# Single-bank PSUM ring, output pieces 18 slices behind and later recurrent reads in a cross-attention and ReGLU kernel

## The chip, the cores and the metric

The kernel runs on one core of a Trainium2 chip. The profiles call the engines PE (TensorE, the matmuls; PEld are its weight loads), ACT (ScalarE), DVE (VectorE), POOL (GpSimd) and SP (SyncE). PSUM is the memory into which the matmuls of this kernel write; ACT and DVE copy the results from there. The metric is the device time of one execution in microseconds, as the median of the runs. The span that the profile gives is about 2 us shorter than the time of the same run. Ratios use runs in the fast state alone; medians and ranges are over all runs of a kernel, of which one in experiment 3 (272.96 us, the split copies) was in the slow state.

## The reference, cut to what matters

```python
# x: 8 batches, 8 heads, 512 tokens, 64 wide; state: 8 batches, 8 heads, 32 slots, 64 wide
a     = softmax(x @ state.T / 8)     ; xread = a  @ state     # 512 tokens read the state
a2    = softmax(state @ x.T / 8)     ; sread = a2 @ x         # 32 slots read the tokens
rows  = concat(xread, sread)         # heads joined: 8 * 544 rows of 512
out   = (relu(rows @ w_gate) * (rows @ w_val)) @ w_out        # 512 -> 1536 -> 512
```

Both kernels avoid `xread` itself: they form U = state @ w_gate and state @ w_val per batch, so that `rows @ w_gate` becomes `a @ U`. Per batch there are

- 12 **slices**: 128 columns of d_ff, two matmuls for gate and two for val, each 128x512; then a relu on ACT and a product on DVE (`h_sb`);
- 12 **pieces**: four 128x512 matmuls each; three pieces make one output tile of 128 rows;
- **units**: scores and their normalisation, transposes, U blocks, and the recurrent reads (`sr`).

## The kernel before

Both kernels allot eight banks of PSUM. In the old one they are a ring of three tiles of two banks, one output bank, and one bank for everything else. A tile is handed on as a whole: its next user waits until the last reader of the tile is done, as the waits below show.

```python
    ps_gv = pool("ps_gv", 3, PS)          # 3 tiles [128, 2, 512]: slices, U, xT, stT
    ps_o = pool("ps_o", 1, PS)            # output tiles
    ps_m = pool("ps_m", 1, PS)            # scores, recurrent reads, aT and srT transposes
    ...
    def gv(b, jf):
        ...
        ps = ps2("gv_ps")                 # gate in ps[:, 0], val in ps[:, 1]
    ...
    def u_block(b, lo, engs=("act", "dve")):
        u_alloc(b)
        for w in range(2):
            ps = ps2("up")
            u_mm(ps, b, w, lo, 512)
            copy[engs[w]](out=U[b][:, w, :, lo:lo + 512], in_=ps)    # 1024 columns at once
    ...
    # startup, in this order on TensorE
    sr0 = sr_mm(0, 0)                     # a recurrent read, held in a PSUM tile until sr_norm
    state_prep(2, 5)
    u_chunk(0, 0)
    u_chunk(1, 0, "dve")
    sr_norm(0, 0, sr0)
    att_aT_pe(0, 0, "act")                # needs the single bank of sr0
    ...
    gv_full(0, 0)
    ...                                   # all 24 slices of batches 0 and 1, then:
    for s in range(2, B + 1):             # stage s: slices of batch s, pieces of batch s-2
        ...
        if n < B:                         # n = s + 1: units of the next batch
            for i, jf in enumerate((3, 5, 7, 9, 10)):
                u.setdefault(jf, []).append(lambda i=i: att_unit_dma(n, i))
            for i, jf in enumerate((4, 6, 8)):
                u.setdefault(jf, []).append(lambda i=i: u_block(n, 512 * i))
```

The softmax here doesn't subtract the row's maximum and nothing guards it: scores larger than these inputs give would overflow.

## Time and profile before

| | before |
|---|---|
| median of three runs | 270.2 us (268.87 to 270.82) |
| span in the profile | 270.1 us |
| first slice starts | 17.4 us |
| first output piece | 68.2 us |
| pitch of stages 3 to 6 | 26.24 us |

The starts of slices in this document are counted: a slice has four weight loads from U, and the timeline lists every weight load. The pitch is the distance between the first slices of two batches. The profiled run is another one, of 271.92 us, with a mean granted clock of 0.975.

From the page of the old kernel, the parts on engines and on forty slices of the span (busy tenths; PEclk is the granted clock in tenths):

```profile
span 270.1 us, 4360 instructions
...
PE 231.8 (86%) x1759; PEld 113.7 (42%) x1790; DVE 140.6 (52%) x250; ACT 129.2 (48%) x215; POOL 25.5 (9%) x36
...
PE   7656667786599788889988998899889999999993
...
PEclk9958889999889999999999999999999999999999
...
```

PE is nearly full in the second half and far from it in the first third. The clock drops in the third of these forty slices and again later.

The waits of PE (who waited for whom: us, times, longest), first from 0 to 82 us, then from 82 to 250 us:

```profile
...
PE gv_ps L279 <- ACT U L269: 4.8, 4, 1.2
PE xT_ps L166 <- ACT xT L169: 2.9, 4, 0.8
PE aT_ps L206 <- DVE br L239: 2.6, 1, 2.6
PE aT_ps L206 <- DVE sr_sb L225: 2.5, 1, 2.5
...
```

```profile
...
PE gv_ps L279 <- DVE h_sb L299: 9.3, 11, 1.0
...
```

The first list holds two kinds of waits for PSUM. `xT` waits for a copy of the other half of its own two-bank tile. `aT` waits for whoever holds the single bank: at 15.83 us for the recurrent read, at 71.84 us for `br`. The timeline at the first of these (start, duration, engine, line, operation, tiles, and in brackets the idle time before and what ended it):

```profile
...
13.75 1.21 DVE L269 CAST U<-upc 128x1024 bf16<-128x1024 f32 x1
...
15.06 0.71 DVE L225 TENSOR_SCALAR sr_sb<-sr_ps,rr 64x128 bf16<-64x128 f32 x2
...
15.83 0.61 PE L206 MATMUL aT_ps<-id_94,a_sn 128*128 128x128 bf16 x4 [2.53 <-DVE sr_sb L225]
...
```

The read's normalisation stands behind a U copy of 1.21 us on DVE, and PE stands still for 2.53 us; the copy, a reciprocal and the normalisation itself fill 2.0 us of them. The clock falls as well. These are windows of 2 us with their granted clock (the column after POOL):

```profile
...
core 0: us, PE busy (x) PEld busy (x) DVE busy (x) ACT busy (x) POOL busy (x), PEclk, DMA share, GB/s
...
12.00:14.00 2.00, 1.08 (x38) 0.71 (x38) 1.93 (x6) 0.26 (x2) 0.74 (x2) 1.00 1.45 196
14.00:16.00 2.00, 0.17 (x2) 0.17 (x3) 1.73 (x4) 1.45 (x3) 1.14 (x2) 0.71 1.45 195
16.00:18.00 2.00, 1.78 (x10) 1.09 (x10) 0.00 (x0) 0.82 (x2) 1.08 (x2) 0.50 1.45 198
...
```

In the stages, the timeline shows one kind of gap only, next to a U block:

```profile
...
138.76 0.69 DVE L190 TENSOR_TENSOR a_sn<-e_sn,rc 128x512 bf16<-128x512 bf16 x1
138.96 0.40 PE L254 MATMUL up<-wv_sb,stT 64*32 64x512 bf16 x8
139.22 1.01 ACT L262 CAST U<-up 128x1024 bf16<-128x1024 f32 x1 [0.64 <-PE up L254]
...
139.36 0.69 DVE L299 TENSOR_TENSOR h_sb<-gv_ps,g_sb 128x512 bf16<-128x512 f32 x1
...
140.10 1.02 PE L279 MATMUL gv_ps<-ans,U 128*128 128x512 bf16 x4 [0.74 <-DVE h_sb L299]
...
```

The U block took two of three tiles. The next slice needs the third, which held the slice before, and that is free only after its product (139.36 to 140.05 us), which stood behind a normalisation on DVE (138.76). A stage has two such gaps, 0.74 us here and 0.99 us at the next U block.

### The profile page before, as it was taken

Reading aid. Unit: us, or ns where it says so; the run is one execution under the profiler, and the core shown is the slowest. Engines: PE = TensorE matmul, PEld = TensorE weight load, DVE = VectorE, ACT = ScalarE, POOL = GpSimd, SP = SyncE. Lnnn points to the kernel's source line nnn. Section 1 sums busy time; section 2 is a strip of 40 time slices with the busy share of each in tenths; the row PEclk is TensorE's granted clock in tenths of the full one; section 3 lists DMA queues with packets and bytes.
Section 4 is the critical chain, followed back from the end, with each engine's and each line's share of the span. In section 5 each row is a group of like instructions: output and inputs, shape, how many; then the busy total and the mean of one; then the engine's idle time right before and its main releaser. Section 6 shows DMA issues by size and latency. Waiting matters only on the chain.

```text
span 270.1 us, 4360 instructions
## 1 busy us (share of the span) xinstructions
PE 231.8 (86%) x1759; PEld 113.7 (42%) x1790; DVE 140.6 (52%) x250; ACT 129.2 (48%) x215; POOL 25.5 (9%) x36
## 2 busy tenths in 40 slices
PE   7656667786599788889988998899889999999993
PEld 2423323343344343344434444344435444666442
DVE  3634634556556876677467647763776433222000
ACT  3344666664336653554454555455645444333211
POOL 4853002000003002000300020000000000000000
PEclk9958889999889999999999999999999999999999
DMA  7999994000061193139114911641131211111242
GB/s 211 195 196 196 205 242 79 4 0 2 0 187 48 39 188 125 39 88 259 44 41 111 241 41 40 137 60 39 41 78 39 78 41 39 54 67 39 78 119 78
DMA packets 38388, 25.71 MB, mean 95 GB/s; under 512 B 18784, under 2 KB 33888, under 8 KB 38368
## 3 DMA queue, kind: packets, MB, share of 16 engines
q1 hardware_dynamic: 27248, 17.70, 24.4%
q0 software_dynamic: 10256, 6.82, 16.1%
q10 hardware_dynamic: 864, 0.92, 1.2%
q8 instruction: 14, 0.23, 0.4%
q14 instruction: 6, 0.05, 0.1%
HBM read 18.35 MB, written 8.91 MB: 101 GB/s over the span
## 4 chain that ended last, share of the span: by engine, by line
PE 68%; DVE 18%; ACT 11%; issue 2%; DVEq 0%; ACTq 0%
PE o_ps L311 27%; PE gv_ps L279 27%; DVE h_sb L299 6%; PE gvs_ps L289 4%; ACT g_sb L295 4%; DVE a_sn L190 4%; DVE cs L187 4%; ACT e_sn L182 3%; PE sr_ps L214 3%; ACT U L269 2%; PE warm_ps L355 2%; DVE rc L189 1%; ACT xT L169 1%; PE o_ps L337 1%; PE up L254 1%
## 5 line engine op out<-in xcount | busy, mean ns | idle before, releaser
L279 PE MATMUL gv_ps<-ans,U 128*128 128x512 bf16 x359 | 98.6, 389 | 19.0 <-DVE h_sb L299 9.7
L299 DVE TENSOR_TENSOR h_sb<-gv_ps,g_sb 128x512 bf16<-128x512 f32 x96 | 66.3, 691 | 72.2 <-ACT g_sb L295 72.2
L311 PE MATMUL o_ps<-wo_sb,h_sb 128*128 128x512 bf16 x367 | 94.8, 382 | 0.3
L295 ACT ACTIVATE g_sb<-gv_ps 128x512 bf16<-128x512 f32 x96 | 57.3, 597 | 71.0 <-PE gv_ps L279 68.3
L279 PEld LDWEIGHTS <-U 128*128 128x128 bf16 x384 | 35.2, 99 | 60.3 <-issue 21.7
L311 PEld LDWEIGHTS <-h_sb 128*128 128x128 bf16 x372 | 36.5, 99 | 40.8 <-issue 0.7
L319 ACT COPY o_sb<-o_ps 128x512 f32<-128x512 f32 x31 | 18.2, 586 | 16.5 <-PE o_ps L311 16.5
L262 DVE CAST U<-up 128x1024 bf16<-128x1024 f32 x18 | 21.9, 1218 | 1.2 <-PE up L254 0.6
L146 POOL CAST xb<-xf 128x1024 bf16<-128x1024 f32 x10 | 10.1, 1041 | 123.9 <-DMA xf<-in_x_dram 123.9
L262 ACT CAST U<-up 128x1024 bf16<-128x1024 f32 x18 | 18.2, 1014 | 7.5 <-PE up L254 7.5
L187 DVE TENSOR_REDUCE cs<-e_sn 128x16 f32<-128x512 bf16 x16 | 10.9, 683 | 6.9 <-ACT e_sn L182 6.9
L299 DVE TENSOR_TENSOR hs_sb<-gvs_ps,g_sb 128x256 bf16<-128x256 f32 x12 | 5.1, 425 | 15.3 <-ACT g_sb L295 15.3
L182 ACT ACTIVATE e_sn<-sc_ps 128x512 bf16<-128x512 f32 x16 | 9.6, 597 | 4.9 <-PE sc_ps L180 4.9
L269 ACT CAST U<-upc 128x1024 bf16<-128x1024 f32 x11 | 11.0, 1015 | 1.8 <-PE upc L254 1.8
L225 DVE TENSOR_SCALAR sr_sb<-sr_ps,rr 64x128 bf16<-64x128 f32 x32 | 11.2, 349 | 0.8
L190 DVE TENSOR_TENSOR a_sn<-e_sn,rc 128x512 bf16<-128x512 bf16 x16 | 11.1, 692 | 0.6
L214 PE MATMUL sr_ps<-xb,e_sn 128*128 128x256 bf16 x64 | 11.3, 278 | 0.0
L295 ACT ACTIVATE g_sb<-gvs_ps 128x256 bf16<-128x256 f32 x12 | 4.6, 384 | 12.0 <-PE gvs_ps L289 12.0
L254 PEld LDWEIGHTS <-stT 64*32 64x32 bf16 x480 | 4.6, 89 | 11.6 <-issue 11.1
L216 PE MATMUL sr_ps<-ones,e_sn 128*128 128x1 bf16 x64 | 9.4, 168 | 0.0
L340 DVE COPY o_sb<-o_ps 128x256 f32<-128x256 f32 x1 | 0.4, 424 | 16.3 <-PE o_ps L337 16.3
L254 PE MATMUL up<-wg_sb,stT 64*32 64x512 bf16 x144 | 7.4, 386 | 0.9 <-DVE h_sb L299 0.9
(61 smaller groups left out, 150.1 us busy)
## 6 DMA issues: line engine op xcount, KB each, us to landing
out_dram<-o_sb SPq DMA_DIRECT2D x31, 256.0 KB, 2.3
xf<-in_x_dram SPq DMA_DIRECT2D x4, 1024.0 KB, 6.5
wg_sb<-in_moe_w_gate_dram POOLq DMA_DIRECT2D x6, 256.0 KB, 10.0
wv_sb<-in_moe_w_val_dram POOLq DMA_DIRECT2D x6, 256.0 KB, 10.1
wo_sb<-in_moe_w_out_dram POOLq DMA_DIRECT2D x2, 768.0 KB, 16.1
xb<-in_x_dram POOLq DMA_DIRECT2D x2, 512.0 KB, 9.4
xf<-in_x_dram POOLq DMA_DIRECT2D x1, 1024.0 KB, 18.8
xf<-in_x_dram ACTq DMA_DIRECT2D x1, 512.0 KB, 4.4
```

The lines of the kernel that those rows point to most:

```text
L182: nc.scalar.activation(out=e_sn[b][:, kc].rearrange("p c m -> p (c m)"), in_=t, func=AF.Exp, scale=scale)
L187: nc.vector.reduce_sum(out=cs, in_=e_v, axis=AX.X)
L190: nc.vector.tensor_tensor(out=a_sn[b][:, kc].rearrange("p c (h n) -> p (c h) n", n=Ns), in0=e_v, in1=rc.to_broadcast([128, NC * HK, Ns]), ...
L214: nc.tensor.matmul(ps[:, 0:256], e_sn[b][:, kc, c], xb[b][:, c, HK * kc:HK * kc + HK], start=(c == 0), stop=(c == NC - 1), skip_group_chec ...
L254: nc.tensor.matmul(ps[q:q + 32, kc, 0:n], stT[r:r + 64, b, j, 32 * sl:32 * sl + 32], wsb[r:r + 64, j, lo:lo + n], start=True, stop=True)
L262: copy[engs[w]](out=U[b][:, w, :, lo:lo + 512], in_=ps)
L269: copy[eng](out=U[b][:, :, :, lo:lo + 256].rearrange("p w k f -> p k w f"), in_=ps)
L279: nc.tensor.matmul(ps[:, w], U[b][:, w, kc, f0:f0 + 128], ANS[b][:, kc].rearrange("p c t -> p (c t)"), start=(kc == 0), stop=(kc == NK - 1))
L295: nc.scalar.activation(out=g_sb[:, 0:n], in_=ps[:, 0, 0:n], func=AF.Relu)
L299: nc.vector.tensor_tensor(out=dst, in0=ps[:, 1, 0:n], in1=g_sb[:, 0:n], op=ALU.mult)
L311: nc.tensor.matmul(o_ps[0], src[:, jf, tsub * 128:(tsub + 1) * 128], wo_sb[:, jf], start=(jf == 0), stop=(jf == NF - 1))
L319: nc.scalar.copy(out=o_sb, in_=o_ps[0])
```

## The change

The intent: one stream of slices in which pieces follow 18 slices behind, with no break between startup and stages; PSUM as a ring of six single banks and two output banks, so that a bank comes free as soon as its one reader is done; and recurrent reads of the first batches moved to stage 2, where DVE has time. The U copies are split, as a tile is now one bank. The exponentials of the scores (`e_sn`) get a third buffer, as the reads that use them come later. The loads of batch 0 come in quarters, and the rest of the state comes later. The diff, cut to its core:

```diff
-    ps_gv = pool("ps_gv", 3, PS)
-    ps_o = pool("ps_o", 1, PS)
-    ps_m = pool("ps_m", 1, PS)
+    ps_r = pool("ps_r", 6, PS)
+    ps_o = pool("ps_o", 2, PS)
...
-        ps = ps2("gv_ps")
+        ps = [bank("gv_ps"), bank("gv_ps")]
...
-    def u_block(b, lo, engs=("act", "dve")):
+    def u_block(b, lo, engs=("act", "act", "dve", "dve")):
...
-            copy[engs[w]](out=U[b][:, w, :, lo:lo + 512], in_=ps)
+            for kc in range(NK):
+                copy[engs[2 * w + kc]](out=U[b][:, w, kc, lo:lo + 512], in_=ps[kc])
...
-    state_dma(nc.sync, 2, B)
...
+        if i == 2:
+            state_dma(nc.gpsimd, 2, B)
...
-    sr0 = sr_mm(0, 0)                      # and the other reads of batches 0 and 1
...
+    first, lag = NF + 6, 18
+    at(2, 1, sr_unit, 0, 0)
+    at(2, 2, sr_unit, 0, 1)
+    at(2, 3, sr_unit, 1, 0)
+    at(2, 4, sr_unit, 1, 1)
...
+    for b in range(3, B):
+        s = b - 1
+        for i, jf in enumerate((7, 8)):
+            at(s, jf, att_unit_dma, b, i)
+        for i, jf in enumerate((6, 8, 10)):
+            at(s, jf, u_block, b, 512 * i)
...
+    for g in range(first, NF * (B + 1)):
+        b, jf = divmod(g, NF)
+        ps, dst, n = gv(b, jf) if b < B else gvs(jf)
+        h_mult(ps, h_relu(ps, n), dst, n)
+        if g >= lag:
+            ob, i = divmod(g - lag, NF)
+            out_piece(ob, i)
+        for f in units.get(g, ()):
+            f()
```

More of the change, by code (lines that the diff above doesn't have):

```diff
@@ L78, with bank @@
     copy = {"act": nc.scalar.copy, "dve": nc.vector.tensor_copy, "pool": nc.gpsimd.tensor_copy}
-    def ps2(name):
-        return ps_gv.tile([128, 2, 512], FP32, name=name, tag="gv")
-    def psm(name):
-        return ps_m.tile([128, 512], FP32, name=name, tag="m")
+    def bank(name, o=False):
+        if o:
+            return ps_o.tile([128, 512], FP32, name=name, tag="o")
+        return ps_r.tile([128, 512], FP32, name=name, tag="r")
     def slot(j, parity):
@@ L124, in state_conv, with state_prep @@
         copy[conv](out=st_b[:, lo:hi], in_=st_f[:, lo:hi])
-    def state_prep(lo, hi):
+    def state_prep(lo, hi, o=False):
         n = hi - lo
-        t = ps2("stT_ps").bitcast(BF16)
-        ps = t.rearrange("p s f -> p (s f)")[0:64, 0:n * 256].rearrange("p (b k m) -> p b k m", b=n, k=NK)
+        ps = bank("stT_ps", o).bitcast(BF16)[0:64, 0:n * 256].rearrange("p (b k m) -> p b k m", b=n, k=NK)
         for bb in range(n):
@@ L158, in x_trans_pe @@
             xT_alloc(b)
-        t = ps2("xT_ps").bitcast(BF16)
         for jj in range(2):
             j = 2 * kc + jj
-            ps = t[:, jj, 0:512].rearrange("p (c t) -> p c t", c=NC)
+            ps = bank("xT_ps").bitcast(BF16)[:, 0:512].rearrange("p (c t) -> p c t", c=NC)
             for c in range(NC):
@@ L169, in x_trans_pe, with att_sc @@
             copy[engs[jj]](out=xT[b][:, :, j], in_=ps)
-    def att_sc(b, kc, wide=False):
+    def att_sc(b, kc, o=False):
         if kc == 0:
-            e_sn[b] = att.tile([128, NK, NC, HK * Ns], BF16, name="e_sn", tag="e_sn")
+            e_sn[b] = att.tile([128, NK, NC, HK * Ns], BF16, name="e_sn", tag="e_sn", bufs=3)
             a_sn[b] = att.tile([128, NK, NC, HK * Ns], BF16, name="a_sn", tag="a_sn")
-        t = ps2("sc_ps")[:, 0] if wide else psm("sc_ps")
+        t = bank("sc_ps", o)
         ps = t.rearrange("p (c j m) -> p c j m", c=NC, j=2)
@@ L199, in att_aT_dma, with att_aT_pe @@
                                     in_=a_sn[b].rearrange("p k c m -> p (k c m)"))
-    def att_aT_pe(b, kc, eng):
+    def att_aT_pe(b, kc, eng, o=False):
         if kc == 0:
             ans_alloc(b)
-        ps = psm("aT_ps").bitcast(BF16)[:, 0:512].rearrange("p (c t) -> p c t", c=NC)
+        ps = bank("aT_ps", o).bitcast(BF16)[:, 0:512].rearrange("p (c t) -> p c t", c=NC)
         for c in range(NC):
@@ L207, in att_aT_pe, with sr_mm @@
         copy[eng](out=ANS[b][:, kc], in_=ps)
-    def sr_mm(b, kc, wide=False):
+    def sr_mm(b, kc, o=False):
         if kc == 0:
             sr_sb[b] = small.tile([128, NK, 128], BF16, name="sr_sb", tag="sr_sb")
-        ps = ps2("sr_ps")[:, 0] if wide else psm("sr_ps")
+        ps = bank("sr_ps", o)
         for c in range(NC):
@@ L226, in sr_norm, with att_sr, att_srT @@
                                         scalar1=rr[r0:r0 + 64])
-    def att_sr(b, kc, wide=False):
-        sr_norm(b, kc, sr_mm(b, kc, wide))
-    def att_srT(b):
-        ps = psm("srT_ps").bitcast(BF16)
+    def att_sr(b, kc, o=False):
+        sr_norm(b, kc, sr_mm(b, kc, o))
+    def att_srT(b, o=False):
+        ps = bank("srT_ps", o).bitcast(BF16)
         for kc in range(NK):
@@ L244, in u_alloc, with u_mm @@
             U[b] = upool.tile([128, 2, NK, d_ff], BF16, name="U", tag="U")
-    def u_mm(ps, b, w, lo, n):
+    def u_mm(dst, b, w, lo, n):
         wsb = (wg_sb, wv_sb)[w]
@@ L253, in u_mm, with u_chunk @@
                     q = 64 * j2 + 32 * sl
-                    nc.tensor.matmul(ps[q:q + 32, kc, 0:n], stT[r:r + 64, b, j, 32 * sl:32 * sl + 32],
+                    nc.tensor.matmul(dst[kc][q:q + 32], stT[r:r + 64, b, j, 32 * sl:32 * sl + 32],
                                      wsb[r:r + 64, j, lo:lo + n], start=True, stop=True)
-    def u_block(b, lo, engs=("act", "dve")):
+    def u_block(b, lo, engs=("act", "act", "dve", "dve")):
         u_alloc(b)
         for w in range(2):
-            ps = ps2("up")
+            ps = [bank("up"), bank("up")]
             u_mm(ps, b, w, lo, 512)
-            copy[engs[w]](out=U[b][:, w, :, lo:lo + 512], in_=ps)
-    def u_chunk(b, lo, eng="act"):
+            for kc in range(NK):
+                copy[engs[2 * w + kc]](out=U[b][:, w, kc, lo:lo + 512], in_=ps[kc])
+    def u_chunk(b, lo, engs=("act", "dve")):
         u_alloc(b)
-        ps = ps2("upc").rearrange("p k (w f) -> p k w f", w=2)
+        ps = [bank("upc").rearrange("p (w f) -> p w f", w=2) for kc in range(NK)]
         for w in range(2):
-            u_mm(ps[:, :, w], b, w, lo, 256)
-        copy[eng](out=U[b][:, :, :, lo:lo + 256].rearrange("p w k f -> p k w f"), in_=ps)
+            u_mm([p[:, w] for p in ps], b, w, lo, 256)
+        for kc in range(NK):
+            copy[engs[kc]](out=U[b][:, :, kc, lo:lo + 256], in_=ps[kc])
     def gv(b, jf):
@@ L275, in gv @@
         f0 = jf * 128
-        ps = ps2("gv_ps")
+        ps = [bank("gv_ps"), bank("gv_ps")]
         for w in range(2):
             for kc in range(NK):
-                nc.tensor.matmul(ps[:, w], U[b][:, w, kc, f0:f0 + 128], ANS[b][:, kc].rearrange("p c t -> p (c t)"),
+                nc.tensor.matmul(ps[w], U[b][:, w, kc, f0:f0 + 128], ANS[b][:, kc].rearrange("p c t -> p (c t)"),
                                  start=(kc == 0), stop=(kc == NK - 1))
@@ L284, in gvs @@
         f0 = jf * 128
-        ps = ps2("gvs_ps")
+        ps = [bank("gv_ps"), bank("gv_ps")]
         nt = B * Ns
@@ L288, in gvs @@
             for j in range(NJ):
-                nc.tensor.matmul(ps[:, w, 0:nt], wsb[:, j, f0:f0 + 128], br[:, j].rearrange("p b n -> p (b n)"),
+                nc.tensor.matmul(ps[w][:, 0:nt], wsb[:, j, f0:f0 + 128], br[:, j].rearrange("p b n -> p (b n)"),
                                  start=(j == 0), stop=(j == NJ - 1))
@@ L294, in h_relu @@
         g_sb = gpool.tile([128, 512], BF16, name="g_sb", tag="g_sb")
-        nc.scalar.activation(out=g_sb[:, 0:n], in_=ps[:, 0, 0:n], func=AF.Relu)
+        nc.scalar.activation(out=g_sb[:, 0:n], in_=ps[0][:, 0:n], func=AF.Relu)
         return g_sb
     def h_mult(ps, g_sb, dst, n):
-        nc.vector.tensor_tensor(out=dst, in0=ps[:, 1, 0:n], in1=g_sb[:, 0:n], op=ALU.mult)
+        nc.vector.tensor_tensor(out=dst, in0=ps[1][:, 0:n], in1=g_sb[:, 0:n], op=ALU.mult)
     def gv_full(b, jf):
@@ L305, with out_mms @@
     o_ps = [None]
-    def out_mms(src, tsub, jfs, wide=False):
+    def out_mms(src, tsub, jfs):
         if jfs[0] == 0:
-            o_ps[0] = ps2("o_ps")[:, 0] if wide else ps_o.tile([128, d_model], FP32, name="o_ps", tag="o")
+            o_ps[0] = bank("o_ps", True)
         for jf in jfs:
@@ L330, in out_last @@
     def out_last(b, tsub):
-        ps = ps2("o_ps")
         n = d_model // 2
@@ L335, in out_last, with out_piece @@
             cols = slice(n * half, n * half + n)
+            ps = bank("o_ps", True)[:, 0:n]
             for jf in range(NF):
-                nc.tensor.matmul(ps[:, half, 0:n], hsb[b][:, jf, tsub * 128:(tsub + 1) * 128], wo_sb[:, jf, cols],
+                nc.tensor.matmul(ps, hsb[b][:, jf, tsub * 128:(tsub + 1) * 128], wo_sb[:, jf, cols],
                                  start=(jf == 0), stop=(jf == NF - 1))
             o_sb = opool.tile([128, d_model], FP32, name="o_sb", tag="o_sb")
-            eng(out=o_sb[:, 0:n], in_=ps[:, half, 0:n])
+            eng(out=o_sb[:, 0:n], in_=ps)
             q.dma_start(out=out_rows(b, tsub)[:, cols], in_=o_sb[:, 0:n])
-    def out_piece(b, i, wide=False):
+    def out_piece(b, i):
         tsub, q = divmod(i, 3)
-        out_mms(hsb[b], tsub, list(range(4 * q, 4 * q + 4)), wide)
+        out_mms(hsb[b], tsub, list(range(4 * q, 4 * q + 4)))
         if q == 2:
@@ L352, in spin @@
     def spin(n):
-        wps = ps_o.tile([128, 512], FP32, name="warm_ps", tag="o")
+        wps = bank("warm_ps", True)
         for i in range(n):
@@ L363 @@
     state_dma(nc.sync, 0, 2)
-    x0_dma(nc.scalar, 0, 4)
-    x0_dma(nc.sync, 4, 8)
+    x0_dma(nc.scalar, 0, 2)
+    x0_dma(nc.sync, 2, 4)
+    x0_dma(nc.scalar, 4, 6)
+    x0_dma(nc.sync, 6, 8)
     nc.scalar.activation(out=tiny, in_=nc.const_aps.tensor(0.0, (128, 1), FP32), func=AF.Exp)
-    state_dma(nc.sync, 2, B)
     make_identity(nc, id128)
@@ L382 @@
     x_dma(3, (nc.gpsimd,))
-    spin(8)
-    state_conv(0, 2, "dve")
-    state_prep(0, 2)
-    x_conv(0, 0, "dve")
-    spin(4)
-    x_trans_pe(0, 0)
-    x_conv(0, 1, "dve")
-    spin(2)
-    att_sc(0, 0, wide=True)
-    x_trans_pe(0, 1, ("dve", "act"))
-    att_norm(0, 0)
-    spin(2)
-    att_sc(0, 1, wide=True)
-    state_conv(2, 5, "act")
-    att_norm(0, 1)
-    sr0 = sr_mm(0, 0)
-    state_prep(2, 5)
-    u_chunk(0, 0)
-    u_chunk(1, 0, "dve")
-    sr_norm(0, 0, sr0)
-    att_aT_pe(0, 0, "act")
@@ L405 @@
-    spin(2)
-    att_aT_pe(0, 1, "act")
-    gv_full(0, 0)
-    gv_full(0, 1)
-    x_trans_pe(1, 0)
-    x_trans_pe(1, 1)
-    att_sr(0, 1)
-    u_chunk(0, 256)
-    gv_full(0, 2)
-    att_sc(1, 0)
-    gv_full(0, 3)
-    att_norm(1, 0)
-    att_sc(1, 1)
-    u_chunk(1, 256)
-    att_norm(1, 1)
-    u_chunk(0, 512)
-    gv_full(0, 4)
-    gv_full(0, 5)
-    att_aT_pe(1, 0, "act")
-    u_chunk(1, 512)
-    att_aT_pe(1, 1, "act")
-    gv_full(1, 0)
-    gv_full(1, 1)
-    u_chunk(0, 768)
-    gv_full(0, 6)
@@ L430 @@
-    gv_full(0, 7)
-    att_srT(0)
-    u_chunk(1, 768)
-    gv_full(1, 2)
-    gv_full(1, 3)
-    u_chunk(0, 1024)
-    gv_full(0, 8)
-    gv_full(0, 9)
-    u_chunk(1, 1024)
-    gv_full(1, 4)
-    gv_full(1, 5)
-    att_sr(1, 0)
-    u_chunk(0, 1280)
-    gv_full(0, 10)
-    gv_full(0, 11)
-    u_chunk(1, 1280)
-    gv_full(1, 6)
-    gv_full(1, 7)
-    att_sr(1, 1)
-    x_trans_pe(2, 0)
-    gv_full(1, 8)
-    x_trans_pe(2, 1)
-    gv_full(1, 9)
-    state_conv(5, B, "pool")
-    att_sc(2, 0)
@@ L455 @@
-    att_norm(2, 0)
-    gv_full(1, 10)
-    state_prep(5, B)
-    att_sc(2, 1)
-    att_norm(2, 1)
-    gv_full(1, 11)
-    u_block(2, 0)
-    att_srT(1)
-    def att_unit_dma(b, i):
-        if i < 2:
-            att_sc(b, i)
-            att_norm(b, i)
-            if i == 1:
-                att_aT_dma(b)
-        elif i < 4:
-            att_sr(b, i - 2)
-        else:
-            att_srT(b)
-    def stage(s, pre=0, units={}):
-        for i in range(pre):
-            out_piece(s - 2, i)
-            for f in units.get(i - pre, ()):
-                f()
-        for jf in range(NF):
-            ps, dst, n = gv(s, jf) if s < B else gvs(jf)
-            g_sb = h_relu(ps, n)
-            if jf + pre < NF:
-                out_piece(s - 2, jf + pre)
-            h_mult(ps, g_sb, dst, n)
-            for f in units.get(jf, ()):
-                f()
@@ L493, in x_next @@
         x_trans_dma(b)
-    for s in range(2, B + 1):
-        u = {}
-        n = s + 1
-        if s == 2:
-            u[-4] = [lambda: att_aT_pe(2, 0, "act")]
-            u[-3] = [lambda: att_aT_pe(2, 1, "dve"), lambda: x_next(3)]
-            u[-2] = [lambda: att_sr(2, 0)]
-            u[-1] = [lambda: u_block(2, 512), lambda: x_dma(4, (nc.sync,))]
-            u[0] = [lambda: att_sr(2, 1)]
-            u[1] = [lambda: u_block(2, 1024)]
-            u[2] = [lambda: att_srT(2)]
-        if n < B:
-            for i, jf in enumerate((3, 5, 7, 9, 10)):
-                u.setdefault(jf, []).append(lambda i=i: att_unit_dma(n, i))
-            for i, jf in enumerate((4, 6, 8)):
-                u.setdefault(jf, []).append(lambda i=i: u_block(n, 512 * i))
-            if n + 1 < B:
-                u.setdefault(6, []).append(lambda: x_next(n + 1))
-            if n + 2 < B:
-                u.setdefault(7, []).append(lambda: x_dma(n + 2, (nc.sync,)))
-        stage(s, pre=4 if s == 2 else 0, units=u)
@@ L516 @@
-    for i in range(3):
-        out_piece(B - 1, i, wide=True)
+    spin(8)
+    state_conv(0, 2, "dve")
+    state_prep(0, 2)
+    spin(3)
+    x_conv(0, 0, "dve")
+    x_trans_pe(0, 0)
+    x_conv(0, 1, "dve")
+    spin(3)
+    att_sc(0, 0, True)
+    x_trans_pe(0, 1, ("dve", "act"))
+    att_norm(0, 0)
+    spin(2)
+    att_sc(0, 1, True)
+    u_chunk(0, 0, ("act", "act"))
+    att_norm(0, 1)
+    spin(2)
+    att_aT_pe(0, 0, "act", True)
+    u_chunk(1, 0, ("act", "act"))
+    x_trans_pe(1, 0, ("dve", "act"))
@@ new lines @@
+    att_aT_pe(0, 1, "dve", True)
+    x_trans_pe(1, 1, ("act", "dve"))
+    gv_full(0, 0)
+    att_sc(1, 0, True)
+    u_chunk(0, 256, ("act", "act"))
+    att_norm(1, 0)
+    gv_full(0, 1)
+    att_sc(1, 1, True)
+    att_norm(1, 1)
+    gv_full(0, 2)
+    u_chunk(1, 256, ("act", "act"))
+    att_aT_pe(1, 0, "act", True)
+    gv_full(0, 3)
+    u_chunk(0, 512)
+    att_aT_pe(1, 1, "act", True)
+    gv_full(1, 0)
+    gv_full(1, 1)
+    u_chunk(1, 512)
+    gv_full(1, 2)
+    gv_full(0, 4)
+    u_chunk(0, 768)
@@ new lines, with att_unit_pe @@
+    gv_full(0, 5)
+    gv_full(1, 3)
+    u_chunk(1, 768)
+    gv_full(0, 6)
+    gv_full(0, 7)
+    u_chunk(0, 1024)
+    gv_full(1, 4)
+    gv_full(1, 5)
+    u_chunk(0, 1280)
+    gv_full(0, 8)
+    gv_full(0, 9)
+    u_chunk(1, 1024)
+    gv_full(0, 10)
+    gv_full(0, 11)
+    u_chunk(1, 1280)
+    def att_unit_pe(b, i):
+        if i < 2:
+            x_trans_pe(b, i)
+        elif i < 4:
+            att_sc(b, i - 2)
+            att_norm(b, i - 2)
+        else:
+            att_aT_pe(b, i - 4, ("act", "dve")[i - 4])
@@ new lines, in att_unit_dma, with sr_unit, at @@
+    def att_unit_dma(b, i):
+        att_sc(b, i)
+        att_norm(b, i)
+        if i == 1:
+            att_aT_dma(b)
+    def sr_unit(b, i):
+        if i < 2:
+            att_sr(b, i)
+        else:
+            att_srT(b)
+    units = {}
+    def at(b, jf, f, *args):
+        units.setdefault(NF * b + jf, []).append(lambda: f(*args))
+    first, lag = NF + 6, 18
+    for i in range(6):
+        at(1, 6 + i, att_unit_pe, 2, i)
+    at(1, 6, state_conv, 2, 4, "pool")
+    at(1, 7, state_prep, 2, 4)
@@ new lines @@
+    at(1, 7, state_conv, 4, B, "pool")
+    at(1, 8, u_block, 2, 0)
+    at(1, 10, u_block, 2, 512)
+    at(2, 0, u_block, 2, 1024)
+    at(2, 1, sr_unit, 0, 0)
+    at(2, 2, sr_unit, 0, 1)
+    at(2, 2, x_next, 3)
+    at(2, 2, x_dma, 4, (nc.sync,))
+    at(2, 3, sr_unit, 1, 0)
+    at(2, 4, sr_unit, 1, 1)
+    at(2, 5, state_prep, 4, B)
+    at(2, 6, sr_unit, 0, 2)
+    for b in range(3, B):
[4 more added lines that the diff above has]
+            at(s, jf, u_block, b, 512 * i)
+        if b + 1 < B:
+            at(s, 9, x_next, b + 1)
+        if b + 2 < B:
+            at(s, 10, x_dma, b + 2, (nc.sync,))
@@ L518 @@
+    for b in range(2, B):
+        for i, jf in enumerate((1, 2, 4)):
+            at(b, jf + (2 if b == 2 else 0), sr_unit, b, i)
+    at(2, 8, sr_unit, 1, 2)
+    for g in range(first, NF * (B + 1)):
[7 more added lines that the diff above has]
+            f()
     for t2 in range(2):
-        out_mms(hs_sb, t2, list(range(NF)), wide=True)
+        out_mms(hs_sb, t2, list(range(NF)))
@@ L520 @@
         fin_s(t2)
-    for i in range(3, 9):
-        out_piece(B - 1, i, wide=True)
+    for i in range(NF - lag % NF, NF - 3):
+        out_piece(B - 1, i)
     out_last(B - 1, NC - 1)
```

## The prediction

> **What bounds the kernel now.** TensorE. Of the 270.1 us span the page has PE busy 231.8 us, ACT 129.2, DVE 140.6. The time falls into two parts:
>
> - 0 to 82 us (table of windows): PE busy only 59.2 us. The list of waits for PE in this stretch: U casts on ACT 4.8 us, `sr_sb` normalisation 2.5 and `br` copy 2.6 (each through the single `ps_m` bank, whose next user is an `aT` transpose), transposes `xT` waiting for the copy of the other half of the same two-bank tile 4.1, `a_sn` 2.0. The granted clock falls to about 0.5 at 16 to 21, 32 to 35 and 73 to 76 us; there 128x512 matmuls start every 0.43 us instead of 0.216. This is what the Trainium skill ("TensorE: Matmul & The Clock Gate", Part 1) calls the cold state after about 3.4 us of low activity. The steady gv/o alternation starts near 77.7 us.
> - 82 to 250 us: PE nearly full. Its only notable wait is gv_ps for the DVE product h_sb (ring of three double banks): 9.3 us in 11 waits. A middle stage takes 26.24 us (start of the same slice at 140.10, 166.35, 192.59), of which I count 24.3 us of matmul pitch.
>
> **What the change removes, adds, moves.** The PE instruction count stays 3582. Removed: false waits inside two-bank tiles, the single `ps_m` bank, recurrent reads of batches 0 and 1 from the startup (four units of 0.53 us, with DVE work of about 0.9 us each), and the break near 66 to 78 us. Moved: output pieces start after 18 slices rather than 24; U chunks run two slices ahead of use; the late state load leaves the head of the DMA stream. Added: U evictions become twice as many 128x512 copies: ACT 2x0.59 for 1.01 us, DVE about 2x0.69 for 1.22, about 6 us on each engine, off the path on average.
>
> **Sum** (estimates from those durations).
> 1. First slice: about 14.5 to 15.5 us, before 17.5 to 18.4, and I expect its matmuls warm or nearly so.
> 2. From there to slice 18: 18x0.87 + 10 chunks x0.5 + attention = 21.7 us on PE, with ACT (20.3) and DVE (20.7) just as full; so about 25 us. The stream starts near 40 us.
> 3. Stream of 90 slice/piece pairs with all units: 181 us of PE pitch. Stalls 6 to 10 us: less ring waiting, because the gate bank frees after the relu; but DVE queues up at slices 6 to 10 (two norms of 1.62 us plus U copies), and the transposed weights (3.2 us by DMA) are asked for only three slices after the last norm, with about 0.5 us to spare.
> 4. Tail: 14.5 us for state rows, three pieces, last tile, copy and store.
>
> 40 + 181 + 8 + 15 = 245 us. Nearly all the gain (about 22 us) lies before 80 us, on the critical path; stages gain below 1 us each.
>
> **Prediction: 246 us, 80% range 239 to 255.** Faster by over 2%: 0.96; within 2%: 0.03; slower: 0.01.
>
> **What would show it.** Windows: PE busy in 15 to 80 us over 85%, hardly any half-clock window after 25 us; first o_ps piece near 40 us (before 68.2). Waits: no aT_ps wait for sr_sb or br; xT waits gone; gv_ps on h_sb from 9.7 to about 6 us. Stage pitch 25 to 26 us. ACT and DVE busy each up some 5 us.
>
> **What would make it wrong.** Startup bound by ACT/DVE queues (stream at 46 us or later); w_out or x1 landing late; gv_ps waiting 1 us or more per stage for the ans transpose; stage 2, with four more recurrent reads, stalling; cold clock again at the start.

## More of the kernel before

Runs of one call share a chip and the runs of the old kernel beside them.

## The result, and the profile after

The new kernel takes 242.7 us (240.96 to 243.57, four runs) against 269.54 us beside it. The ratio is 0.8991 (95% interval 0.8926 to 0.9056). Ratios here are the mean time of one kernel's fast runs over that of the other's of the same rounds, so not quite the ratio of the medians quoted. Executions over 1.5% slower than the fastest of the same kernel are left out of the means.

| slice k starts at, us | 0 | 12 | 24 | 36 | 48 | 84 | state rows' output | span |
|---|---|---|---|---|---|---|---|---|
| before | 17.4 | 46.8 | 77.7 | 103.3 | 129.6 | 208.3 | 252.5 | 270.1 |
| after | 16.5 | 33.1 | 54.0 | 84.0 | 108.8 | 183.2 | 225.9 | 240.3 |

At slice 36 the new kernel is 19.3 us ahead and has also six more pieces behind it (18 against 12 are due there). A piece is 0.86 us in the chain of waits, so the lead is worth 24.5 us. Stages 3 to 6 add 1.44 us each (24.80 for 26.24), which makes 5.8 us. The sum, 30.3 us, is within half a microsecond of the 29.8 us between the two spans. These are spans of one run each, though: the medians lie only 26.8 us apart. The old kernel's profiled run was a long one. In two more profiles with the ring of three (experiment 3) the pitch is the same 26.24 us, so the 3 us lie probably before slice 36. By the medians the lead there is then nearer 21.5 us (an estimate: 26.8 less 5.8, plus the half microsecond).

The page after:

```profile
span 240.3 us, 4513 instructions
...
PE 225.1 (94%) x1758; PEld 111.3 (46%) x1790; DVE 145.7 (61%) x276; ACT 123.5 (51%) x236; POOL 26.7 (11%) x38
...
PE   7768899998999999999999999999999999999993
...
PEclk9979999999999999999999999999999999999999
...
```

The waits of PE, first from 0 to 45 us, then from 45 to 240 us:

```profile
...
PE xT_ps L162 <- DMA xb<-in_x_dram: 2.7, 1, 2.7
...
PE gv_ps L278 <- ACT ans L203: 0.8, 1, 0.8
...
```

```profile
...
PE gv_ps L278 <- ACT e_sn L178: 1.5, 4, 0.4
PE gv_ps L278 <- DVE ans L203: 1.2, 1, 1.2
...
```

No wait for `h_sb`, `sr_sb`, `br` or a U copy is left. The new one is the first: PE waits 2.7 us for the load of batch 1, and soon after that it runs at half clock (mean granted clock 0.50 from 16 to 18 us).

```profile
...
11.27 0.29 PE L251 MATMUL upc<-wv_sb,stT 64*32 64x256 bf16 x8
14.30 0.70 PE L162 MATMUL xT_ps<-id_91,xb 128*64 128x128 bf16 x16 [2.75 <-DMA xb<-in_x_dram]
...
15.48 1.06 PE L162 MATMUL xT_ps<-id_91,xb 128*64 128x128 bf16 x16
16.48 1.46 PE L278 MATMUL gv_ps<-ans,U 128*128 128x512 bf16 x3
...
```

How full PE is can also be read from the windows of U alone (the second number in brackets is weight loads, four for each slice). Before, then after:

```profile
...
0.00:40.00 40.00, 11.01 (x30) 3.45 (x32) 1.21 (x1) 5.17 (x6) 0.87 1.24 210
...
```

```profile
...
0.00:40.00 40.00, 18.09 (x69) 6.55 (x75) 4.77 (x7) 8.88 (x16) 0.96 1.22 205
...
```

In the first 40 us the loads went from 32 to 75, that is from 8 slices to almost 19.

### The profile page after: what moved, and what is told of

Same layout as the page of the kernel before. It is cut to its first block, busy times and chain, and to the rows that moved or that the text cites. A ratio compares the mean times of both kernels' runs of the same rounds, so it can differ in the third digit from the quotient of the medians.

```text
span 240.3 us, 4513 instructions
## 1 busy us (share of the span) xinstructions
PE 225.1 (94%) x1758; PEld 111.3 (46%) x1790; DVE 145.7 (61%) x276; ACT 123.5 (51%) x236; POOL 26.7 (11%) x38
## 4 chain that ended last, share of the span: by engine, by line
PE 80%; DMA 6%; DVE 5%; ACT 4%; issue 2%; POOL 1%; ACTq 0%
PE o_ps L310 34%; PE gv_ps L278 33%; PE gv_ps L288 4%; DMA xb<-in_x_dram 3%; PE sr_ps L210 3%; PE up L251 2%; ACT o_sb L318 2%; DVE h_sb L298 2%; ACT e_sn L178 2%; DMA st_f<-in_state_dram 1%; PE xT_ps L162 1%; DVE cs L183 1%; DVE U L260 1%; PE upc L251 1%; DMA out_dram<-o_sb 1%
## 5 line engine op out<-in xcount | busy, mean ns | idle before, releaser
L278 PE MATMUL gv_ps<-ans,U 128*128 128x512 bf16 x367 | 96.6, 381 | 4.3 <-ACT e_sn L178 1.5
L310 PE MATMUL o_ps<-wo_sb,h_sb 128*128 128x512 bf16 x359 | 93.1, 379 | 0.6
L294 ACT ACTIVATE g_sb<-gv_ps 128x512 bf16<-128x512 f32 (+1 forms) x108 | 62.6, 580 | 52.8 <-PE gv_ps L278 38.1
L278 PEld LDWEIGHTS <-U 128*128 128x128 bf16 x384 | 33.8, 98 | 44.8 <-issue 13.2
L260 DVE CAST U<-up 128x512 bf16<-128x512 f32 x36 | 23.1, 684 | 3.0 <-PE up L251 2.4
L260 ACT CAST U<-up 128x512 bf16<-128x512 f32 x36 | 19.4, 594 | 10.2 <-PE up L251 10.2
L298 DVE TENSOR_TENSOR hs_sb<-gv_ps,g_sb 128x256 bf16<-128x256 f32 x12 | 5.1, 425 | 15.3 <-PE gv_ps L288 10.5
L221 DVE TENSOR_SCALAR sr_sb<-sr_ps,rr 64x128 bf16<-64x128 f32 x32 | 11.2, 350 | 0.8
L268 ACT CAST U<-upc 128x512 bf16<-128x512 f32 x16 | 9.2, 609 | 1.2 <-PE upc L251 1.2
L176 PEld LDWEIGHTS <-xT 128*128 128x128 bf16 x128 | 5.9, 98 | 4.6 <-ACT xT L165 0.6
L354 PE MATMUL warm_ps<-warm 128*128 128x512 bf16 x17 | 6.1, 494 | 1.2 <-DVE warm L356 1.2
```

The costliest lines, as they stand in the source:

```text
L221: nc.vector.tensor_scalar_mul(out=sr_sb[b][r0:r0 + 64, kc], in0=ps[r0:r0 + 64, 128 * j2:128 * j2 + 128], scalar1=rr[r0:r0 + 64])
L260: copy[engs[2 * w + kc]](out=U[b][:, w, kc, lo:lo + 512], in_=ps[kc])
L278: nc.tensor.matmul(ps[w], U[b][:, w, kc, f0:f0 + 128], ANS[b][:, kc].rearrange("p c t -> p (c t)"), start=(kc == 0), stop=(kc == NK - 1))
L294: nc.scalar.activation(out=g_sb[:, 0:n], in_=ps[0][:, 0:n], func=AF.Relu)
L298: nc.vector.tensor_tensor(out=dst, in0=ps[1][:, 0:n], in1=g_sb[:, 0:n], op=ALU.mult)
L310: nc.tensor.matmul(o_ps[0], src[:, jf, tsub * 128:(tsub + 1) * 128], wo_sb[:, jf], start=(jf == 0), stop=(jf == NF - 1))
```

## The experiments

Three theories stood at the start. **Both matter:** the new order fills PE in the startup, the new banks shorten the stages. **Order alone:** the stream gives nearly everything. **Banks alone:** the ring gives nearly everything. All runs were correct.

### 1. New order, old banks

```diff
-    ps_r = pool("ps_r", 6, PS)
-    ps_o = pool("ps_o", 2, PS)
+    ps_gv = pool("ps_gv", 3, PS)    # slices, U, xT, stT as pairs; U copies stay split
+    ps_o = pool("ps_o", 1, PS)
+    ps_m = pool("ps_m", 1, PS)      # scores, reads, aT, srT
```

> The new order of work in the old PSUM layout (ring of three two-bank tiles, one output bank, one bank for the rest); U copies stay split in four. Theory (both halves matter, and what the banks give lies in the stages): about 253 us, stage pitch back from 24.8 to about 26.2 us, PE waits for the product h_sb back to about 9 us. Rival 1 (the order gives all, the banks are decoration): at most 244 us and a pitch of about 24.8. Rival 2 (the banks give nearly all): over 262 us.

Measured: 251.37 us (250.03 to 253.68), ratio 0.9303 (0.9239 to 0.9367). The total fits "both", but my number for the pitch was wrong: 25.0 us, not 26.2. With the old banks the new order takes 1.2 us off a stage; which part of the order does it was not separated. The waits for `h_sb` were 5.4 us, not the 9 that I expected. What the old banks cost lies elsewhere: slices 12 to 36 took 57.2 us instead of 50.9 (34.2 to 91.4 us, against 33.1 to 84.0). Its waits of PE:

```profile
...
PE gv_ps L284 <- DVE h_sb L304: 5.4, 14, 1.5
PE sr_ps L216 <- DVE sr_sb L227: 2.1, 2, 1.0
...
```

### 2. Old order, new banks

```diff
-    ps_gv = pool("ps_gv", 3, PS)
-    ps_o = pool("ps_o", 1, PS)
-    ps_m = pool("ps_m", 1, PS)
+    ps_r = pool("ps_r", 6, PS)      # everything but output tiles, one bank each
+    ps_o = pool("ps_o", 2, PS)      # order of work as before; U copies split per bank
```

> The old order of work with the new PSUM layout (ring of six single banks, two output banks, U copies split per bank). Theory: about 256 us; the waits of the xT and aT transposes go (about 9 us), the stage pitch falls to about 24.8, but output pieces still start near 60 us and the waits for U on ACT stay. Rival 1 (order gives all): 266 us or more. Rival 2 (banks give nearly all): 246 us or less.

Measured: 245.95 us (245.36 to 246.89), ratio 0.9097 (0.9058 to 0.9136). This just meets the mark of "banks alone" (246 or less; the runs lie on both sides of it) and misses my 256. Pieces still start at 56 us and the recurrent reads still stand in the startup, yet 24 of 27 us are there. The first slice starts at 13.75 us with the clock at 1.00, and the pitch is 24.52 us, better than the 24.80 of the new kernel. As expected, waits for U remain; no wait of a slice for `h_sb` is in the list:

```profile
...
PE gv_ps L276 <- ACT U L266: 3.6, 4, 1.6
...
```

So each half alone gives most of the gain: 24.2 us (banks) and 18.8 us (order), both from the medians beside 270.18 us. Together they give about 27, so some 16 us can be had either way.

### 3. Which part of the banks?

Three runs on the old order took the bank change apart. The first has only the ring split:

```diff
-    ps_gv = pool("ps_gv", 3, PS)    # two-bank tiles
+    ps_r = pool("ps_r", 6, PS)      # single banks; ps_o 1 and ps_m 1 stay as they were
```

> The old kernel in its old order; only its ring of three two-bank tiles becomes six single banks (U copies split per bank). The single output bank and the single bank for scores, reads and transposes stay. Theory (two separate costs: two-bank tiles cost the xT waits and the 1.7 us per stage; the shared single bank costs the blocked aT transposes and the cold clock after them): between the old kernel and 246 us, about 254, stage pitch about 24.5 us, aT waits for sr_sb and br still there. Rival (the two-bank tiles are the whole cost): at most 248 us.

Measured: 252.09 us (251.87 to 252.35), ratio 0.9300 (0.9243 to 0.9357). The theory holds: 252 us for "about 254", pitch 24.52 us, and these waits are still there:

```profile
...
PE gv_ps L280 <- ACT U L270: 6.6, 6, 2.1
PE aT_ps L205 <- DVE br L238: 2.7, 1, 2.7
PE aT_ps L205 <- DVE sr_sb L224: 2.6, 1, 2.6
...
```

The same place as in the old kernel, after a U block, in the timeline:

```profile
...
123.35 0.59 ACT L296 ACTIVATE g_sb<-gv_ps 128x512 bf16<-128x512 f32 x1
...
124.49 0.69 DVE L189 TENSOR_TENSOR a_sn<-e_sn,rc 128x512 bf16<-128x512 bf16 x1
124.70 0.40 PE L253 MATMUL up<-wv_sb,stT 64*32 64x512 bf16 x8
...
125.03 1.12 PE L280 MATMUL gv_ps<-ans,U 128*128 128x512 bf16 x4
125.10 0.68 DVE L300 TENSOR_TENSOR h_sb<-gv_ps,g_sb 128x512 bf16<-128x512 f32 x1
...
```

DVE is as late as before: the product runs at 125.10 to 125.78 us, behind the same normalisation. But the next slice starts at 125.03, before it, right behind the U block. Its first matmul needs only the gate bank, which the relu on ACT freed at 123.94 us; in the old kernel it needed the whole tile and so waited for DVE. The val bank is asked for two matmuls later. The fall of the pitch, 1.72 us (26.24 to 24.52), is about the sum of the two gaps of an old stage, 0.74 and 0.99 us.

The second gives up the single bank instead and keeps tiles of two banks:

```diff
-    ps_o = pool("ps_o", 1, PS)
-    ps_m = pool("ps_m", 1, PS)
+    ps_o = pool("ps_o", 2, PS)      # users of ps_m take a two-bank tile of the ring of three
```

> The old kernel in its old order; two-bank tiles stay, but the single bank for scores, reads and transposes is given up: its users take a two-bank tile from the ring of three, and the output gets a second bank. Theory: the aT waits for sr_sb and br go and the first slice comes near 14 us, but the xT waits and the stage pitch (26.2 us or more) stay: about 262 us. Rival (the shared bank is the whole cost): at most 250 us.

Measured: 268.8 us (267.57 to 269.94), ratio 0.9915 (0.9841 to 0.9990), within 2% of the old kernel. I had expected 262 us. The waits of `aT` for `sr_sb` and `br` are gone, but others have come: the first slice still starts at 17.1 us (I had expected 14), the pitch stays at 26.24 us, and the ring of three is now asked for more.

```profile
...
PE gv_ps L278 <- DVE h_sb L298: 11.7, 15, 1.6
...
PE xT_ps L165 <- ACT xT L168: 3.0, 4, 0.8
PE gv_ps L278 <- DVE a_sn L189: 1.4, 1, 1.4
PE upc L253 <- ACT stT L137: 1.4, 1, 1.4
...
```

So the two parts of the bank change are not a sum. Giving up the single bank is worth little while a tile costs two banks. On top of the split it is worth 6 us (252.1 to 246.0; ratios 0.9300 and 0.9097). Whenever the single bank was given up, the output got a second one; the two were not separated.

The third tests a rival for the split. Splitting the ring also splits the U copies, and shorter copies alone might have been the help:

```diff
-            copy[engs[w]](out=U[b][:, w, :, lo:lo + 512], in_=ps)
+            for kc in range(NK):
+                copy[engs[w]](out=U[b][:, w, kc, lo:lo + 512], in_=ps[:, kc])   # u_chunk likewise
```

> The old kernel, two-bank tiles and all, with the U copies split per bank (512 columns each) and nothing else. Theory (what helped in the split-only run is that banks come free one by one, not that copies are shorter): pitch 26.2 us or more, total 268 to 274 us. Rival (the shorter copies are what helped): pitch at most 25.2 us, total at most 260 us.

Measured: 270.97 us (268.59 to 272.96), ratio 0.9947 (0.9876 to 1.0018), pitch 26.24 us. The rival falls: the waits for `h_sb` are those of the old kernel (9.7 us in 13 waits over the whole run).

```profile
...
PE gv_ps L281 <- DVE h_sb L301: 9.7, 13, 1.0
...
```

The Trainium skill ("Perfetto Trace Analysis", Optimizing Scalar/DVE Operations) says that breaking up instructions on an engine that is not saturated may let work finish sooner. Here it changed nothing that can be measured while the tiles kept their two banks.

### 4. Places of the units in the stages

```diff
+        old = b > 3
-        for i, jf in enumerate((7, 8)):
+        for i, jf in enumerate((3, 5) if old else (7, 8)):
             at(s, jf, att_unit_dma, b, i)
-        for i, jf in enumerate((6, 8, 10)):
+        for i, jf in enumerate((4, 6, 8) if old else (6, 8, 10)):
             at(s, jf, u_block, b, 512 * i)
+        if old:                             # recurrent reads in the same stage again
+            for i, jf in enumerate((7, 9, 10)):
+                at(s, jf, sr_unit, b, i)
```

> The new kernel, but in stages 3 to 6 attention, U blocks and recurrent reads stand at the slices where the old kernel had them (3 and 5; 4, 6, 8; 7, 9, 10, in the same stage). Theory (the pitch comes from the banks): pitch stays within 0.3 us of 24.8, total within 1.5 us of the new kernel. Rival (the pitch comes from the new places): pitch about 26 us, total 4 to 6 us more.

Measured: 242.74 us (241.32 to 243.15), ratio 0.8958 (0.8912 to 0.9003). The total is that of the new kernel. The pitch is 24.52 us, so with single banks the old places are even 0.28 us better; only the stage that takes the reads of two batches is longer (26.03 us). From slice 36 to the end this run is 0.8 us shorter than the new kernel's (155.6 for 156.3 us); its startup is 1.4 us longer, with a mean clock of 0.66 from 12 to 22 us where the new kernel's profile has 0.83. That it comes out even is thus partly the startup of that run. Why the new places cost a little can be seen in the new kernel at slice 8 of a stage, where a U block follows a score tile:

```profile
...
126.61 0.40 PE L176 MATMUL sc_ps<-stT,xT 128*128 128x64 bf16 x8
...
126.94 0.41 PE L251 MATMUL up<-wg_sb,stT 64*32 64x512 bf16 x8
127.17 0.40 PE L251 MATMUL up<-wv_sb,stT 64*32 64x512 bf16 x8
127.30 0.60 ACT L178 ACTIVATE e_sn<-sc_ps 128x512 bf16<-128x512 f32 x1
...
127.95 1.02 PE L278 MATMUL gv_ps<-ans,U 128*128 128x512 bf16 x4 [0.38 <-ACT e_sn L178]
...
```

Scores and U block take five of six banks in a row, and the next slice waits 0.38 us for the exponential of those scores (the four waits for `e_sn` in the list after).

### 5. Pieces 24 behind instead of 18

```diff
-    first, lag = NF + 6, 18
+    first, lag = NF + 6, 24
...
-    for i in range(NF - lag % NF, NF - 3):
+    for i in range(0, NF - 3):
```

> The new kernel with output pieces 24 behind instead of 18: none between slices 18 and 24, six more at the end. Theory (the pieces fill PE while the attention of batch 2 waits for ACT and DVE): 2 to 5 us slower, with PE idle between slices 18 and 24. Rival (starting pieces early only moves work): within 1 us.

Measured: 244.71 us (243.62 to 245.07), ratio 0.9041 (0.9004 to 0.9078). That is 2.0 us over the run of experiment 4, which has the time of the new kernel. The trace shows the exchange: slices 18 to 24 took 11.2 us without pieces and 14.4 us with six of them in the new kernel, so six pieces of 5.2 us cost 3.2 us there. Right after that PE stood still 2.1 us without them, for the transposed weights of batch 2, as I had expected; by slice 36 (42.2 us after slice 18, for 44.4) the six pieces had cost only 2.2 us. At the end the same six pieces cost all of 5.2 us (19.55 us from the state rows to the end, against 14.4 us). The continuous stream as such is worth 2 us by the medians.

### 6. Recurrent reads back in the startup

```diff
+    sr0 = sr_mm(0, 0)          # in place of a spin(2); att_sr(0, 1), att_sr(1, 0), att_sr(1, 1)
+    sr_norm(0, 0, sr0)         # after the first aT; the srT transposes of batch 0 between slices
...
-    at(2, 1, sr_unit, 0, 0)    # and four more; the srT transposes of batch 1 stay in stage 2
```

> The new kernel with the recurrent reads of batches 0 and 1 back in the startup, where the old kernel had them. Theory (DVE is nearly full there, so four reads of about 0.9 us of DVE cost more than the 0.53 us each that leave stage 2 on PE): 1 to 3 us slower. Rival (they only move): within 1 us.

Measured: 241.23 us (240.94 to 242.03), ratio 0.8904 (0.8847 to 0.8960). It is not slower; my expectation of 1 to 3 us was wrong. From the first slice to slice 18 it takes 24.9 us instead of 23.1; from there to slice 36 it takes 42.0 us instead of 44.4. The reads only move. One thing differs from the old kernel: the normalisation of the first read stands here after the first `aT`, not before it. In experiment 2 it stands before, as of old, and the first slice still came at 13.75 us. So in the old kernel the read hurt because it held the one bank that `aT` needed, not because it stood early.

### 7. Slice 0 before the transposes of batch 1

```diff
-    x_trans_pe(1, 0, ("dve", "act"))
     att_aT_pe(0, 1, "dve", True)
+    gv_full(0, 0)
+    x_trans_pe(1, 0, ("dve", "act"))
     x_trans_pe(1, 1, ("act", "dve"))
-    gv_full(0, 0)
```

> The new kernel, but the second aT transpose and slice 0 stand before the transposes of batch 1, which wait until 14.3 us for their load. Theory (PE idles 2.7 us for that load and then runs cold until 18 us): first slice near 13.3 us, no half-clock stretch, 1 to 2.5 us faster. Rival (ACT and DVE bound the startup anyway): within 0.5 us.

Measured: 241.1 us (240.95 to 242.38), ratio 0.8910 (0.8841 to 0.8979). The first slice starts at 12.68 us, and the mean clock is 1.00 (0.992 before). Slice 4 starts at 21.9 us instead of 23.4. The interval overlaps that of the new kernel's ratio, so the 1.6 us between the medians are not shown by this run alone.

### 8. The old loads

```diff
-    x0_dma(nc.scalar, 0, 2)    # quarters, rest of the state later
+    x0_dma(nc.scalar, 0, 4)    # halves, rest of the state at once
+    x0_dma(nc.sync, 4, 8)
+    state_dma(nc.sync, 2, B)
```

> The new kernel with the loads of the old one: batch 0 in two halves, the rest of the state in one piece right behind them. Theory (the order of loads hardly matters, as batch 1 lands near 14.3 us with either): within 1 us of the new kernel, landing of batch 1 within 0.7 us of 14.3. Rival (the state in front delays batch 1 and the weights): 1.5 us or more slower.

Measured: 243.07 us (240.91 to 244.26), beside 243.38 us (243.06 to 245.06) for the new kernel once more on the same chip. No difference is seen. The landing of batch 1 came at 15.3 us here, outside the 0.7 us that I allowed, but it came at 16.0 us in that second run of the new kernel and at 14.3 us in the first. In these three profiles it moves from run to run as much as with the order of the loads. The new kernel's second run also waited 3.0 us for a piece of w_val, which its first did not.

The repeat of the new kernel had this expectation, and confirmed it at ratio 0.8971 (0.8928 to 0.9014):

> The new kernel once more, unchanged, as the yardstick of this set: 242 us.

### 9. A version that takes the better of both

The slice of experiment 7 first, the reads of experiment 6 in the startup (the normalisation of the first one after `aT`), and the scores of batches 4 to 7 at slices 5 and 7:

```diff
-        for i, jf in enumerate((7, 8)):
+        for i, jf in enumerate((5, 7) if b > 3 else (7, 8)):
```

> The new kernel with slice 0 before the transposes of batch 1, the recurrent reads of batches 0 and 1 in the startup, and the scores of batches 4 to 7 at slices 5 and 7 instead of 7 and 8 (so that no U block follows a score tile in the ring at once). If the three gains add up: pitch 24.5 in place of 24.8 us (1.1 us over four stages), first slice near 13.5 us, together 3 to 4 us under the new kernel, about 238.5 us. If they overlap: within 1.5 us of it.

Measured: 240.65 us (239.99 to 241.37, six runs), ratio 0.8859 (0.8819 to 0.8899), against 243.06 to 245.06 us for the new kernel on the same chip. No run of one reaches into those of the other; the gain is 2.7 us between the medians, about 1%. That is less than the 3 to 4 us of three gains that add up, and more than the 1.5 of gains that overlap. The pitch is 24.67 us, not the 24.5 that I expected. Three parts changed at once, so the 2.7 us are not shared out among them. The first slice came at 15.17 us, not near 13.5, for a reason outside the edit: a piece of w_val landed late, and the clock fell.

```profile
...
PE upc L251 <- DMA wv_sb<-in_moe_w_val_dram: 2.4, 1, 2.4
...
```

```profile
...
10.00:12.00 2.00, 0.06 (x8) 0.00 (x0) 1.93 (x4) 0.47 (x1) 2.00 (x3) 0.82 1.26 159
12.00:14.00 2.00, 1.53 (x19) 1.06 (x19) 0.23 (x1) 1.07 (x2) 1.15 (x2) 0.50 1.37 184
...
```

## Why the prediction was right or wrong

**The total was right.** 246 us with a range of 239 to 255 was predicted, 242.7 us measured. (The four terms of the sum add to 244, not 245.) Part of it is luck: the first slice came 1 to 2 us late and the stretch after it was about 1 us shorter than said, so the start of the stream near 40 us came out right from two misses. A cold clock at the start stood among what would make the prediction wrong; it came, and the total held.

- **Step 1, first slice at 14.5 to 15.5 us and nearly warm: wrong.** It came at 16.5 us and cold. I had assumed that the later state load would bring batch 1 earlier. It landed at 14.3 us; in the old kernel a wait of GpSimd for it ended at 14.26 us. PE idled for it until then, and the clock halved at about 14.7 us (an estimate from the mean clock of 0.68 in the window from 14 to 16 us).
- **Step 2, stream near 40 us: right.** The first piece starts at 40.5 us. From slice 6 on PE runs without a gap of over 0.15 us, with two slices and a chunk every 2.17 us; ACT and DVE keep up.
- **Step 3, 181 us of pitch and 6 to 10 us of stalls: the stalls were too many.** From the first piece to the state rows it took 185.6 us (40.3 to 225.9 us, by weight loads), which leaves 4.6 us of stalls if the 181 are right. I expected 6 us of waiting for `h_sb`; there is none. The freed gate bank does more than I gave it, as the run with the split ring alone shows. The fear for the `ans` transpose did not come true: no wait for it by DMA is in the list.
- **"Stages gain below 1 us each": wrong, 1.44 us.** This is step 3 seen from the stages. The smaller stalls (4.6 us for the 8 of the sum) are most of the 3 us by which the time is under the prediction.
- **Step 4, tail of 14.5 us: right**, 14.4 us.
- **"ACT and DVE busy each up some 5 us": half wrong.** DVE rose from 140.6 to 145.7 us, ACT fell from 129.2 to 123.5 us. Two things were missed. Eight half-width chunk copies went to DVE, where one of full width had been. And busy time counts overlapping records once: the durations alone (count times mean) rose on both, from 132.9 to 134.5 us on ACT and from 143.8 to 151.5 us on DVE, but more of them now follow each other without a break, and such neighbours overlap. A pair of 512 columns takes 1.07 us on ACT where one of 1024 took 1.01, and 1.27 for 1.22 us on DVE. I had doubled the duration of one.
- **The reasons were weighed wrongly.** The prediction counted the deferred reads and the earlier pieces among what the gain is made of. The experiments show that putting off the reads is worth nothing here (experiment 6) and the earlier pieces 2 us (experiment 5). The bank layout alone brings the old order to 245.95 us. That most of the gain lies before 80 us stands: 24.5 us by slice 36, of 29.8, in the traces, and about 21.5 of 26.8 by the medians (the estimate above), near the 22 us that were predicted.

What stays open: which part of the new order makes it worth 18.8 us with the old banks. Its 1.2 us per stage are seen; the rest (chunks two slices ahead of their use, no read in front of `aT`) was not taken apart. Nor was the gain of the new banks in the startup shared out among the single waits that went. The 1.6 us of experiment 7 are not settled either.

## What to carry to other kernels

When PE waits for a buffer, ask first how much memory one tile holds until its last reader is done, and split the tile before reordering work: a ring of six single banks beat three pairs by 18.6 us with the same order of work. Giving up the bank reserved for small tiles (and getting a second output bank) was worth 6 us on top of single banks, and about 2 us while tiles kept two: in that bank one user can put the next behind an engine's whole queue, as the waits of 2.5 and 2.6 us show. Two changes that remove the same wait don't add up, so run each alone before crediting either.

## What the Trainium skill lacked or had wrong

- "TensorE: Matmul & The Clock Gate" (Part 1 and its table of practical rules) puts the loss of the full clock at an idle window of about 3.4 us, which does not start with the kernel, and advises no gaps over about 3 us. Here half clock began during or within 0.5 us after gaps of 2.53 us (old kernel), 2.75 us (new) and 2.40 us (experiment 9), which came after some microseconds of sparse work; in the old kernel the mean clock of 0.71 from 14 to 16 us puts the fall at about 14.8 us (an estimate from that mean), some 1.5 us after the last matmul. A gap of 1.2 us (experiment 2) kept it. But the length of one gap does not decide: one of 1.41 us (ending at 14.51 us in the run without the single bank, experiment 3) was followed by a mean clock of 0.54 from 16 to 18 us, and one of 2.11 us (ending at 52.73 us in experiment 5) left the clock at 1.00. What does decide is open here.
- The same page has the cold start right, but the granted clock of the profile does not show it: the windows give 1.00 from 0 to 4 us, while the first eight warm-up matmuls of the old kernel took 3.57 us, over 0.4 us each. (The page warns that the clock events of a trace can be unreliable.)
- "Perfetto Trace Analysis" (Matmul Optimizations) advises to use all eight PSUM banks. The old kernel used all eight and lost 24.2 us against another grouping of the same eight with the same order of work. That page's sentence on consistent bubbles ("can mean there isn't enough SBUF/PSUM for the next tile to be allocated") fits: 9.3 us in 11 waits. The sentence names buffer count and tile sizes; that in this kernel only the last reader of a tile frees its banks, so that a tile with two readers is better split (18.6 us in experiment 3), is on no page.
- The same page (Optimizing Scalar/DVE Operations) gives a fixed cost per instruction on PSUM of about 51 ns for ScalarE and 125 ns for VectorE. A pair of split copies cost 0.06 us more than one whole on ACT, which agrees, and 0.05 us more on DVE, which is less.
